# A gated mix of an S5 scan and an H3 convolution on one core: the order of VectorE's products and sums in the convolution chunks, and the place of the inverse transform

## The chip, the core and the metric

The kernel runs on one core of one Trainium2 chip. The metric is device time in microseconds (us) of one execution, the median of several runs. A profiled execution gives beside it a span: the time from the first to the last instruction that the profile shows. Engines are named as the profile names them: PE (TensorE, matmuls), PEld (its weight loads), DVE (VectorE), ACT (ScalarE), POOL (GpSimd), SP (SyncE, which only issues transfers here).

## What is computed

Two sequence models over the same input x (2048 rows of 1024 channels) are mixed by a gate. Cut to what matters:

```python
g = sigmoid((x * gate_w).sum(-1, keepdims=True))
a = S5(x)       # complex linear recurrence h = Lam_bar*h + Bu, then 2*Re(C h) + x*Dskip
# b: H3, per channel
k_shift = 4-tap causal convolution of k with shift_k
kv = k_shift * v
y  = causal convolution of kv with ssm_k over the 2048 rows   (by FFT of length 4096)
b  = x * (y + kv * ssm_D)
out = g * a + (1 - g) * b
```

The change lies in the long convolution, `y`.

## The kernel before

**Two stages.** The convolution stage goes over the 1024 channels in 8 chunks of 128 (`c` = 0 to 7). In it stand also the first pieces of the S5 part (`Bu`, the products of x with B), put between the convolution's steps. The scan stage follows, with 16 scans on DVE, the products with C on PE, and the output rows.

**One chunk.** The 2048 rows are handled as four blocks of 512 and transformed per block by matmuls with cosine and sine tables. For chunk c there are:

- `taps` (line 571): the four taps as matmuls, evicted by ACT into `ks`; `times_v` (line 601) multiplies `ks` by v on DVE, mirrors half of it by a matmul with a reflection matrix (`mirror`, line 579), has ACT evict that to `lo`, forms the even part `ev = ks - lo` on DVE and the odd part by a copy-add of POOL (`gather`, a transfer that adds to its destination) into `ks`.
- `fwd_K` and `fwd_V` (lines 634, 672): the spectra of the filter and of kv, matmuls into PSUM tiles `psk` and `psv`, evicted by ACT into `BT` (the filter's spectrum, K) and `Vh` (V).
- `products` (line 685): the product of the two spectra block by block, so that block a of K meets blocks 0 to 3-a of V. The sum is `A`, which lies in `sums` (named acc in the profile): `A[k, c, b, x]` with k the part of K, c the part of V, b the output block and x 512 frequency-channel pairs. Then the complex combination, and two sums into `whole[c]` (named Vh), which take V's place.
- `inverse` (line 753): for each half `par`, 8 matmuls with the tables CI and SI into a PSUM tile `psz`, an eviction `cv` on ACT, and a store of it to device memory by SP.

**products in detail, chunks 1 to 6.** It is a generator; each `yield` is a place where the main loop goes on with other work. Its steps on DVE:

1. `first(0)`: A[0] = K0 * V, 4096 elements for each partition.
2. `second(0)`: 3072 elements into `WK` (wkh in the profile), and a copy-add of POOL that adds them to A[0].
3. `first(1)`: A[1], 4096.
4. `second(1)`: 3072 into WK.
5. A[1] += that (line 723), 3072.
6. `n2` (4096, into `WK[:, 3072:7168]`, which overlaps what step 5 reads) and `n3` (2048, into a tile `t`).
7. n2 += n3 (2048); A[1] += n2[1] (2048).
8. A[0] += n2[0] (2048).
9. A[1,1] = A[0,0] - A[1,1] and A[1,0] = A[0,1] + A[1,0] (2048 each), then the two sums into `whole[c]` (2048 each).

Chunk 7 runs the same steps without POOL's copy-add, from line 1324; chunk 0 has its own halves.

**What sets the order.** Every instruction is recorded through `put` (line 92), which keeps the order of the program on each engine, so all engines work strictly in the order in which the generators are stepped. `step(g)` runs one piece, `steps(g, n)` n pieces, `run(g)` the rest. All such instructions carry line 94 in the profile, so they are told apart by the names of their tiles. A wait for an earlier instruction of the same engine is a semaphore wait like any other.

**The loop around the change** (lines 1184 to 1197), with c the chunk whose products are formed, n = c + 1 the one whose mirror and `ev` are formed, and c - 1 the one that is transformed back:

```python
step(old); step(tabs)          # turn tables of the S5 part, ACT (c <= 4; old: c 2 to 5)
step(back)                     # first half of inverse(c-1): PE, ACT, store
step(tv)                       # mirror(n) on PE, lo on ACT
steps(prod, 3)                 # first(0), second(0), first(1)
run(tv)                        # ev on DVE, copy-add into ks on POOL
step(prod)                     # second(1)
step(old); step(tabs)
run(back)                      # second half of inverse(c-1)
run(old)
```

`ks` of chunk n is multiplied by v at the end of the turn before (line 1254), right behind the sums into `whole[c-1]`. PSUM has four tiles of two banks, taken in turn by everything that is multiplied.

Of the kernel before, what the change touches and what calls it, by code (L numbers as in the profile page):

```python
# [9 lines left out]
ALU = mybir.AluOpType  # L10
ACT = mybir.ActivationFunctionType
BF16 = mybir.dt.bfloat16
# [8 lines left out]
def kernel(  # L21
# [70 lines left out]
    def put(eng, f, *a, **kw):  # L92
        with tc.issue_after(prev[eng]) if eng in prev else nullcontext():
            i = f(*a, **kw)  # L94
        prev[eng] = getattr(i, "ins", i)
# [4 lines left out]
    def bc(ap, shape):  # L100
        return ap.to_broadcast(shape)
# [3 lines left out]
    def tt(o, a, b, op):  # L105
        put("dve", V.tensor_tensor, out=o, in0=a, in1=b, op=op)
# [19 lines left out]
    def gather(o, i):  # L126
        put("pool", nc.gpsimd.dma_start, out=o, in_=i, accum_op=ALU.add)
# [5 lines left out]
    def h3pool(st, name, bufs, **kw):  # L133
        return st.enter_context(tc.tile_pool(name=name, bufs=bufs, **kw))
# [6 lines left out]
    WK = h3pool(h3, "wkh", 1).tile([128, 7168], BF16, name="wkh")  # L141
# [543 lines left out]
    def products(c, h=0, home=u4, by_dma=True):  # L685

        K, Vt = (x[c][h].rearrange("p c b f d -> p c b (f d)") for x in (KH, VH))
        w = K.shape[3]
        A = sums[:, :, h * 2048:h * 2048 + 8 * w].rearrange("p k (c b x) -> p k c b x", c=2, x=w)

        def mult(a, t):

            if len(t.shape) == 2:
                t = t.rearrange("p (k y) -> p k y", k=2)
            t = t.rearrange("p k (c b x) -> p k c b x", c=2, x=w)
            k_ = bc(K[:, :, a:a + 1], [128, 2, 8 - 2 * a, w])
            v_ = bc(Vt[:, :, 0:4 - a].rearrange("p c b x -> p c (b x)")[:, None], [128, 2, 2, (4 - a) * w])
            tt(t, k_, v_, ALU.mult)
            return t

        n1 = WK[:, h * 3072:h * 3072 + 12 * w].rearrange("p (k c b x) -> p k c b x", k=2, c=2, b=3)

        def first(k):

            for f in range(2 if c == 0 and h == 0 else 1):
                x = slice(f * 128, f * 128 + 128) if c == 0 and h == 0 else slice(0, w)
                tt(A[:, k, :, :, x], bc(K[:, k:k + 1, 0:1, x], [128, 2, 4, x.stop - x.start]), Vt[:, :, :, x], ALU.mult)

        def second(k):
            tt(n1[:, k], bc(K[:, k:k + 1, 1:2], [128, 2, 3, w]), Vt[:, :, 0:3], ALU.mult)  # L710

        if by_dma:
            first(0)
            yield
            second(0)
            gather(A[:, 0, :, 1:], n1[:, 0])
            yield
            first(1)
            yield
            second(1)  # L720
            if c > 0:
                yield
            tt(A[:, 1, :, 1:], A[:, 1, :, 1:], n1[:, 1], ALU.add)
        else:
            mult(0, sums)
            yield
            mult(1, WK[:, 0:6144])
            yield
            tt(A[:, :, :, 1:], A[:, :, :, 1:], n1, ALU.add)
        if c > 0:  # L730
            yield
        n2 = mult(2, WK[:, 3072:7168] if c > 0 else home([128, 8 * w], BF16, "t"))
        n3 = mult(3, home([128, 4 * w], BF16, "t"))
        yield
        tt(n2[:, :, :, 1:], n2[:, :, :, 1:], n3, ALU.add)
        tt(A[:, 1, :, 2:], A[:, 1, :, 2:], n2[:, 1], ALU.add)
        yield
        tt(A[:, 0, :, 2:], A[:, 0, :, 2:], n2[:, 0], ALU.add)
        yield
        tt(A[:, 1, 1], A[:, 0, 0], A[:, 1, 1], ALU.subtract)  # L740
        tt(A[:, 1, 0], A[:, 0, 1], A[:, 1, 0], ALU.add)
        if c == 0 and h == 0:
            return
        t2 = sums[:, 1]
        if c > 0:
            lo, hi = (A[:, 1, :, :, i * 256:(i + 1) * 256] for i in range(2))
        else:
            lo, hi = (t2[:, i * 2048:(i + 1) * 2048].rearrange("p (c b x) -> p c b x", c=2, x=256) for i in range(2))
        to = whole[c].rearrange("p (a c b x) -> p a c b x", a=2, c=2, b=4)
        tt(to[:, 0], lo, hi, ALU.subtract)  # L750
        tt(to[:, 1], lo, hi, ALU.add)
# [326 lines left out]
    def step(gen):  # L1078
        next(gen, None)

    def run(gen):
        for _ in gen:
            pass

    def steps(gen, n):
        for _ in range(n):
            step(gen)
# [59 lines left out]
    for c in range(NC - 1):  # L1147
        n, nn = c + 1, c + 2
        if c == 0:
            load("kn", 2)  # L1150
            load("kT", 2)
            load("v", 2)
            load_BT(0, 0)
            load_xT(0, (0,))
            p1 = products(0, 1)
            fwd_K(n, (0, 1))
            steps(p0, 2)
            run(tv)
            dg = dgs(nn, True)
            steps(p1, 2)  # L1160
            step(p0)
            step(p1)
            run(p0)
            taps(nn, dg)
            step(sp)
            fwd_K(n, (2, 3))
            step(p1)
            step(sp)
            fwd_V(n)
            run(p1)  # L1170
            run(fold_K(nn))
            tv = times_v(nn)
            step(tv)
            load("kn", 3)
            load("kT", 3)
            load_BT(0, 1)
            apart = spread(3)
            step(apart)
            load_xT(0, (1,))
            run(apart)  # L1180
            continue
        if c == 6:
            put("pool", nc.gpsimd.tensor_copy, stamp, xTs[2][:, 0, 0:HB + 1:HB])
        tabs, back, prod = turn_table(c - 1) if c <= NG else none, inverse(c - 1), products(c)
        step(old)
        step(tabs)
        if c == 6:
            step(parts)
        step(back)
        step(tv)  # L1190
        steps(prod, 3)
        run(tv)
        step(prod)
        step(old)
        step(tabs)
        run(back)
        run(old)
        fk = none
        if nn < NC:
            dg = dgs(nn)  # L1200
            if by_channel(nn):
                fk = fold_columns(nn)
                step(fk)
        if c == 2:
            step(parts)
        fwd_K(n, (0, 1))
        if c in (2, 6):
            step(parts)
        fwd_K(n, (2, 3))
        if c == 1:  # L1210
            lam_diag(0, lam_pool, True)
        if c == 4:
            step(parts)
        if c == 6:
            run(sp)
            s5p["Q"] = s5p["wu"]
            run(turns_U[2])
            gate(0)
        step(prod)
        if nn < NC:  # L1220
            if not by_channel(nn):
                fk = mirror_K(nn)
            step(fk)
            if c < 5:
                step(fk)
            if c == 4:
                step(parts)
            if c == 1:
                load_BT(1, 0, True)
            elif c < 5:  # L1230
                load("v", nn, True)
            step(parts)
            taps(nn, dg)
            if c == 5:
                load("v", nn)
                load_xT(2, held=True)
            if nn + 1 < NC:
                load("kT", nn + 1, True)
                load("kn", nn + 1)
                apart = spread(nn + 1)  # L1240
                step(apart)
                if c == 1:
                    load_BT(1, 1)
                elif c in (2, 3):
                    load_xT(1, (3 - c,))
                run(apart)
        step(prod)
        run(fk)
        run(prod)
        if n == NC - 1:  # L1250
            overlap_K(n)
        if nn < NC:
            tv = times_v(nn)
            step(tv)
            step(parts)
        else:
            run(next(tiles))
            CT[0] = ld.tile([128, 2, D], BF16, name="CTa", tag="ld")
            hold(CT[0][:, 0, 0:1])
            load_CT(0)  # L1260
            load_BT(2, 0)
            load_BT(2, 1)
            run(next(tiles))
            run(next(tiles))
        fwd_V(n, (0, 1))
        if c < 6 and c != 4:
            step(parts)
            if c in (1, 3):
                step(parts)
        fwd_V(n, (2, 3))  # L1270
        if c in (4, 5):
            step(parts)
        if c == 1:
            lam_diag(1, lam_pool)
        old = tabs

    h3r.close()
    c = NC - 1
# [38 lines left out]
    with tc.tile_pool(name="fin", bufs=1, side="right") as fin:  # L1317
# [6 lines left out]
        prod, back = products(c, 0, room, False), inverse(c - 1)  # L1324
# [24 lines left out]
    back = inverse(c)  # L1349
# [207 lines left out]
```

## Time and profile before

| | |
|---|---|
| median of 3 runs | 382.99 us (382.91 to 383.02) |
| the profiled execution | 383.41 us |
| its span | 381.6 us |
| granted TensorE clock | 0.997 |
| instructions in the profile | 6664 |

A timeline row gives start, duration, engine, operation, output and inputs by the program's names, their shapes, how many instructions the row stands for, and in brackets the idle time before it and what ended it. Durations of neighbouring instructions may overlap, as their ends are partly modelled; the step from one start to the next is therefore the better measure of what an instruction costs its engine.

### The profile page before, as it was taken

Reading aid. Unit: us, or ns where it says so; the run is one execution under the profiler, and the core shown is the slowest. Engines: PE = TensorE matmul, PEld = TensorE weight load, DVE = VectorE, ACT = ScalarE, POOL = GpSimd, SP = SyncE. Lnnn points to the kernel's source line nnn. Section 1 sums busy time; section 2 is a strip of 40 time slices with the busy share of each in tenths; the row PEclk is TensorE's granted clock in tenths of the full one; section 3 lists DMA queues with packets and bytes.
Section 4 is the critical chain, followed back from the end, with each engine's and each line's share of the span. In section 5 each row is a group of like instructions: output and inputs, shape, how many; then the busy total and the mean of one; then the engine's idle time right before and its main releaser. Section 6 shows DMA issues by size and latency. Waiting matters only on the chain.

```text
span 381.6 us, 6664 instructions
## 1 busy us (share of the span) xinstructions
PE 374.0 (98%) x2469; PEld 201.0 (53%) x2469; DVE 370.8 (97%) x566; ACT 309.5 (81%) x475; POOL 80.3 (21%) x109
## 2 busy tenths in 40 slices
PE   8999999999999999999999999999999999999995
PEld 6656367574674846644454444444444444444434
DVE  8899999999999999999999999999999999999996
ACT  5879998988979998786949999986989669937621
POOL 4011030110301103041002113122415233635000
PEclk9999999999999999999999999999999999999998
DMA  7989999999999998959999999958798999998902
GB/s 167 167 113 260 221 208 185 225 210 223 202 171 197 214 203 188 180 126 154 210 208 209 218 196 210 241 127 143 152 236 162 235 249 229 166 246 142 221 1 110
DMA packets 126259, 71.78 MB, mean 188 GB/s; under 512 B 104649, under 2 KB 107601, under 8 KB 126226
## 3 DMA queue, kind: packets, MB, share of 16 engines
q1 hardware_dynamic: 112416, 45.90, 55.9%
q0 software_dynamic: 12688, 25.17, 39.2%
q8 instruction: 19, 0.31, 0.4%
q10 hardware_dynamic: 1122, 0.28, 0.4%
q14 instruction: 14, 0.11, 0.1%
HBM read 15.48 MB, written 8.39 MB: 63 GB/s over the span
## 4 chain that ended last, share of the span: by engine, by line
DVE 50%; PE 19%; issue 14%; DMA 9%; ACT 5%; POOL 2%; DVEq 0%; POOLq 0%; ACTq 0%
DVE acc L94 14%; DVE wkh L94 9%; PE both L94 9%; DVE A L94 7%; DMA U<-Q 5%; DVE U L94 4%; DMA row<-gd 3%; DVE t L94 3%; DVE trn L94 3%; DVE Vh L94 2%; PE taps L94 2%; PE psz L94 2%; DVE ks L94 2%; ACT Q L94 2%; PE psk L94 2%
## 5 line engine op out<-in xcount | busy, mean ns | idle before, releaser
L94 PE MATMUL psy<-CT,U 128*128 128x512 bf16 (+1 forms) x426 | 93.4, 374 | 0.9 <-DVE U L94 0.9
L94 PEld LDWEIGHTS <-U 128*128 128x128 bf16 x492 | 48.0, 98 | 56.9 <-DVE U L94 1.4
L94 PEld LDWEIGHTS <-BT 128*128 128x128 bf16 x544 | 50.5, 98 | 33.4
L94 ACT ACTIVATE Q<-U,lam 128x512 bf16<-128x512 bf16 (+1 forms) x66 | 39.0, 635 | 15.9 <-DVE U L94 15.9
L94 DVE TENSOR_TENSOR wkh<-BT,Vh 128x3072 bf16<-128x3072 bf16 (+3 forms) x24 | 44.2, 1842 | 0.2
L94 POOL DMA_DIRECT2D U<-Q x26 | 26.1, 1018 | 83.4 <-ACT Q L94 35.7
L94 DVE TENSOR_TENSOR acc<-BT,Vh 128x4096 bf16<-128x4096 bf16 (+3 forms) x19 | 36.9, 1949 | 0.3 <-ACT Vh L94 0.2
L94 PE MATMUL both<-xT,BT 128*128 128x512 bf16 x160 | 35.3, 379 | 0.0
L94 ACT ACTIVATE Vh<-psv 128x1024 bf16<-128x1024 f32 x32 | 30.7, 1032 | 5.5 <-PE psv L94 5.5
L94 ACT ACTIVATE BT<-psk 128x1024 bf16<-128x1024 f32 x31 | 30.3, 1032 | 3.3 <-PE psk L94 3.1
L94 DVE TENSOR_TENSOR acc<-acc,wkh 128x2048 bf16<-128x2048 bf16 (+3 forms) x23 | 32.3, 1431 | 0.5
L94 DVE TENSOR_TENSOR_SCAN A<-rv,init,A 128x256 bf16<-128x256 f32 x48 | 32.2, 731 | 0.0
L94 ACT ACTIVATE U<-both 128x512 bf16<-128x512 f32 x44 | 24.2, 594 | 9.6 <-PE both L94 9.3
L94 POOL DMA_DIRECT2D acc<-wkh x8 | 9.8, 1219 | 103.3 <-DVE wkh L94 103.3
L94 PE MATMUL psk<-eok,SF 128*128 128x384 bf16 (+1 forms) x120 | 28.5, 354 | 0.0
L94 PEld LDWEIGHTS <-SF 128*128 128x128 bf16 x184 | 18.0, 98 | 18.8
L94 PE MATMUL psz<-Vh,CI 128*128 128x512 bf16 x64 | 24.3, 380 | 0.0
L94 PE MATMUL psz<-Vh,SI 128*128 128x512 bf16 x64 | 24.3, 379 | 0.0
L94 PEld LDWEIGHTS <-kT 128*128 128x128 bf16 x352 | 22.2, 103 | 1.3 <-DMA kT<-in_B_k_dram 0.8
L94 PE MATMUL taps<-dg,kT 128*128 128x128 bf16 (+1 forms) x352 | 22.6, 216 | 0.0
L94 PE MATMUL both<-xT,BTl 128*128 128x512 bf16 x96 | 21.2, 379 | 0.0
L94 PE MATMUL both<-BT,BT 128*128 128x512 bf16 x96 | 21.0, 379 | 0.0
(223 smaller groups left out, 770.1 us busy)
## 6 DMA issues: line engine op xcount, KB each, us to landing
U<-Q POOLq DMA_DIRECT2D x26, 256.0 KB, 5.1
acc<-wkh POOLq DMA_DIRECT2D x6, 768.0 KB, 8.6
cv_scr<-cv SPq DMA_DIRECT2D x16, 256.0 KB, 7.5
kn<-in_B_ssm_k_dram SPq DMA_DIRECT2D x5, 512.0 KB, 4.8
v<-in_B_v_dram SPq DMA_DIRECT2D x5, 512.0 KB, 6.1
out_dram<-m SPq DMA_DIRECT2D x8, 256.0 KB, 4.4
BT<-cv_scr SPq DMA_DIRECT2D x7, 256.0 KB, 7.5
out_dram<-BT SPq DMA_DIRECT2D x7, 256.0 KB, 2.0
```

The costliest lines, as they stand in the source:

```text
L94: i = f(*a, **kw)
```

## The change

In `products`, for chunks 1 to 7, steps 6 to 8 are reordered and three instructions are issued in halves: n3 comes ahead of n2; n2's product, the sum n2 += n3, and A[0] += n2[0] are each made as two instructions, one for each k or each c. In the loop, both halves of the inverse now come ahead of the mirror, and `second(1)` comes ahead of `ev`.

```diff
-        n2 = mult(2, WK[:, 3072:7168] if c > 0 else home([128, 8 * w], BF16, "t"))
-        n3 = mult(3, home([128, 4 * w], BF16, "t"))
-        yield
-        tt(n2[:, :, :, 1:], n2[:, :, :, 1:], n3, ALU.add)
-        tt(A[:, 1, :, 2:], A[:, 1, :, 2:], n2[:, 1], ALU.add)
-        yield
-        tt(A[:, 0, :, 2:], A[:, 0, :, 2:], n2[:, 0], ALU.add)
-        yield
+        if c > 0:
+            n3 = mult(3, home([128, 4 * w], BF16, "t"))
+            n2 = WK[:, 3072:7168].rearrange("p (k c b x) -> p k c b x", k=2, c=2, b=2)
+            for k in (1, 0):
+                tt(n2[:, k], bc(K[:, k:k + 1, 2:3], [128, 2, 2, w]), Vt[:, :, 0:2], ALU.mult)
+            yield
+            for k in (1, 0):
+                tt(n2[:, k, :, 1:], n2[:, k, :, 1:], n3[:, k], ALU.add)
+            tt(A[:, 1, :, 2:], A[:, 1, :, 2:], n2[:, 1], ALU.add)
+            yield
+            for i in (0, 1):
+                tt(A[:, 0, i, 2:], A[:, 0, i, 2:], n2[:, 0, i], ALU.add)
+            yield
+        else:
...
         tt(A[:, 1, 1], A[:, 0, 0], A[:, 1, 1], ALU.subtract)
         tt(A[:, 1, 0], A[:, 0, 1], A[:, 1, 0], ALU.add)
...
-        step(back)
+        run(back)
         step(tv)
-        steps(prod, 3)
+        steps(prod, 4)
         run(tv)
-        step(prod)
         step(old)
         step(tabs)
-        run(back)
         run(old)
```

Under `else` chunk 0 keeps the old lines.

More of the change, by code (lines that the diff above doesn't have):

```diff
@@ L731, in products @@
             yield
-        n2 = mult(2, WK[:, 3072:7168] if c > 0 else home([128, 8 * w], BF16, "t"))
-        n3 = mult(3, home([128, 4 * w], BF16, "t"))
-        yield
-        tt(n2[:, :, :, 1:], n2[:, :, :, 1:], n3, ALU.add)
-        tt(A[:, 1, :, 2:], A[:, 1, :, 2:], n2[:, 1], ALU.add)
-        yield
-        tt(A[:, 0, :, 2:], A[:, 0, :, 2:], n2[:, 0], ALU.add)
-        yield
+        if c > 0:
[12 more added lines that the diff above has]
+        else:
+            n2 = mult(2, home([128, 8 * w], BF16, "t"))
+            n3 = mult(3, home([128, 4 * w], BF16, "t"))
+            yield
+            tt(n2[:, :, :, 1:], n2[:, :, :, 1:], n3, ALU.add)
+            tt(A[:, 1, :, 2:], A[:, 1, :, 2:], n2[:, 1], ALU.add)
+            yield
+            tt(A[:, 0, :, 2:], A[:, 0, :, 2:], n2[:, 0], ALU.add)
+            yield
         tt(A[:, 1, 1], A[:, 0, 0], A[:, 1, 1], ALU.subtract)
```

## The prediction

> **What bounds the kernel now.** I read the page's first table, then the list of all waits, then the windows, then the timeline of VectorE (DVE) over one convolution chunk, and last the timelines of the others around the places that the diff moves.
>
> ```profile
> PE 374.0 (98%) x2469; PEld 201.0 (53%) x2469; DVE 370.8 (97%) x566; ACT 309.5 (81%) x475; POOL 80.3 (21%) x109
> ```
> ```profile
> PEld L94 <- DVE ks L94: 4.4, 6, 0.9
> ...
> PE mirror L94 <- DVE ks L94: 1.5, 4, 0.4
> ...
> PEld L94 <- DVE Vh L94: 1.2, 3, 0.5
> PE psy L94 <- DVE U L94: 0.9, 1, 0.9
> ```
> ```profile
> 240.00:270.00 30.00, 30.00 (x140) 13.55 (x139) 29.62 (x64) 25.06 (x39) 6.19 (x8) 1.00 0.82 168
> ```
>
> The reader is to see two full engines. The windows row is one from the second half (stretch and length, then PE, weight load, DVE, ACT and POOL busy): PE 30.00 of 30 us, DVE 29.62. The waits list says which of the two holds the other. Behind the start, DVE has no row in it against another engine; PE has these four against DVE. So DVE sets the end, PE follows it closely, and what counts is whether DVE loses time between its own instructions. It does:
>
> ```profile
> 92.11 1.22 DVE L94 TENSOR_TENSOR ks<-ks,v 128x2048 bf16<-128x2048 bf16 x1
> 93.24 2.29 DVE L94 TENSOR_TENSOR acc<-BT,Vh 128x4096 bf16<-128x4096 bf16 x1
> 95.44 1.75 DVE L94 TENSOR_TENSOR wkh<-BT,Vh 128x3072 bf16<-128x3072 bf16 x1
> 97.11 2.29 DVE L94 TENSOR_TENSOR acc<-BT,Vh 128x4096 bf16<-128x4096 bf16 x1
> 99.32 0.69 DVE L94 TENSOR_TENSOR ev<-ks,lo 128x1024 bf16<-128x1024 bf16 x1
> 99.92 1.75 DVE L94 TENSOR_TENSOR wkh<-BT,Vh 128x3072 bf16<-128x3072 bf16 x1
> 101.71 1.76 DVE L94 TENSOR_TENSOR acc<-acc,wkh 128x3072 bf16<-128x3072 bf16 x1
> 103.50 2.29 DVE L94 TENSOR_TENSOR wkh<-BT,Vh 128x4096 bf16<-128x4096 bf16 x1
> 105.71 1.22 DVE L94 TENSOR_TENSOR t<-BT,Vh 128x2048 bf16<-128x2048 bf16 x1
> 106.96 1.22 DVE L94 TENSOR_TENSOR wkh<-wkh,t 128x2048 bf16<-128x2048 bf16 x1
> 108.22 2.36 DVE L94 TENSOR_TENSOR acc<-acc,wkh 128x2048 bf16<-128x2048 bf16 x2
> 110.62 2.36 DVE L94 TENSOR_TENSOR acc<-acc 128x2048 bf16<-128x2048 bf16 x2
> 113.01 2.36 DVE L94 TENSOR_TENSOR Vh<-acc 128x2048 bf16<-128x2048 bf16 x2
> 115.29 1.22 DVE L94 TENSOR_TENSOR ks<-ks,v 128x2048 bf16<-128x2048 bf16 x1
> ```
>
> This is chunk 3, 23.18 us from ks to ks. Look at starts, not durations. Where the next instruction does not need this one, it starts 0.08 us before this one's end: 3072 elements from 95.44 to 97.11, 1.67 us; 2048 from 92.11 to 93.24, 1.13. Where it does, it starts 0.03 us after the end: 3072 from 99.92 to 101.71, 1.79; 2048 from 105.71 to 106.96, 1.25. **A direct dependence costs 0.12 us**, a loss that no busy column shows. The starts at 101.71, 103.50 (wkh is overwritten while the sum has just read it), 106.96, 108.22, 110.62 and 113.01 are the six such places of the chunk.
>
> **The change, part by part.** *Size of a split.* From 99.32 to 99.92 a 1024-element instruction takes 0.60 us, a 2048 one 1.13: two halves are 1.20, so each split adds 0.07. The diff splits three instructions of 7 chunks (1 to 7): 21 x 0.068 = 1.43 us more on DVE, which nothing hides.
>
> *Gaps closed.* Behind the change ev stands between the second product of wkh and the sum that reads it; t's product stands between that sum and the overwriting of wkh; each half of n2 and each half sum has its sibling between it and its reader; both halves of the last sum into A[0] stand so that A[1,1] reads the older one. Of the six dependent starts only the one into Vh is left. Does one instruction in between suffice? Chunk 5 has that case already:
>
> ```profile
> 152.07 1.22 DVE L94 TENSOR_TENSOR t<-BT,Vh 128x2048 bf16<-128x2048 bf16 x1
> 153.20 0.69 DVE L94 TENSOR_TENSOR eok<-kn,lo 128x1024 bf16<-128x1024 bf16 x1
> 153.81 1.22 DVE L94 TENSOR_TENSOR wkh<-wkh,t 128x2048 bf16<-128x2048 bf16 x1
> ```
>
> wkh<-wkh,t reads t, eok of 1024 elements lies between, and the steps are 1.13 and 0.61: no gap. The shortest instruction between a writer and its reader in the new order is such a 1024 one, so I count these gaps as closed. Chunks 1 to 4 close five each, 0.595; chunk 5 four (one was covered by eok), chunk 6 four (the small state-parameter operations already stood ahead of its sum), chunk 7, which has no ev, four, 0.476 each. Net of the 0.204 for the splits: 4 x 0.39 + 3 x 0.27 = **2.37 us less on DVE**.
>
> The Trainium skill speaks against this ("VectorE: DVE Perf Modes", The DRAIN you can't avoid, and its rules for kernel authors): the next operation waits for the pipe to empty whether or not a semaphore stands between, and one should minimize the count of operations, not of semaphores. The 0.12 us between the two kinds of step disagree with the first half here; the 0.07 per extra instruction agrees with the second. What the change would be if the rule held is a rival below.
>
> *Inverse ahead of the mirror.* PE ahead of chunk 5's mirror, and at the first inverse matmul of chunk 3:
>
> ```profile
> 138.78 0.38 PE L94 MATMUL psz<-Vh,CI 128*128 128x512 bf16 x1
> 139.00 0.38 PE L94 MATMUL psz<-Vh,SI 128*128 128x512 bf16 x1
> 139.75 0.60 PE L94 MATMUL mirror<-ks,refl 128*128 128x512 bf16 x2 [0.37 <-DVE ks L94]
> ```
> ```profile
> 90.51 0.59 PE L94 MATMUL psv<-ks,SF 128*128 128x512 bf16 x2
> 91.11 0.39 PE L94 MATMUL psz<-Vh,CI 128*128 128x512 bf16 x1
> ```
>
> A 512-column matmul takes a slot of 0.22 us (138.78 to 139.00). From 139.00 to 139.75 PE loses 0.53 waiting for ks, of which the row shows 0.37, since a matmul's modelled 0.38 us outlasts its slot by 0.16. The waits list has four such (1.5 us in all on PE) among the six of the weight loads; the other two are hidden in that 0.16. So 4 x 0.53 + 2 x 0.16, about 2.5 us. With both halves of the inverse in front, 16 slots or 3.45 us lie between Vh's first half and the mirror, while ks comes 2 x 1.13 us after that half: the mirror waits no more, and the second Vh half (1.13 after the first) is there when its 8 slots begin. PE also waits for Vh itself 0.17 at 91.11 (two matmuls of 0.22 from 90.51, so it was free at 90.94) which I count twice, 0.3 us, for the list's three waits on Vh; that goes if DVE gains. In all PE can shed 2.8 us.
>
> What is late next on PE? Two things. First, ACT's order becomes cv, cv, lo:
>
> ```profile
> 95.48 1.04 ACT L94 ACTIVATE cv<-psz 128x1024 bf16<-128x1024 f32 x1
> 96.38 1.05 ACT L94 ACTIVATE lo<-mirror 128x1024 bf16<-128x1024 f32 x1
> 97.29 1.06 ACT L94 ACTIVATE cv<-psz 128x1024 bf16<-128x1024 f32 x1
> ```
>
> Four PSUM tiles rotate, so the second psk of fwd_K needs the first cv evicted. Its place is 25 slots or 5.4 us after the first psz (16 psz, 2 mirror, and psk's 4 of 512 and 4 of 384 columns), 96.3 if psz starts at 90.9, and cv ends at 96.5. So some 0.2 us come back in chunk 3, 0.1 in chunk 4, where ACT has the turn tables ahead of cv. For ev nothing changes: lo ends one eviction later, 98.3 instead of 97.4, and ev starts at 100.99 instead of 99.32, since the 1.67 us product passes it.
>
> Second, POOL's copy-add into ks waits for ev, and so is issued 1.67 us later; behind it on POOL stands the turn table's copy-add, used in the next chunk. In chunks 1 and 3:
>
> ```profile
> 50.16 1.20 POOL L94 DMA_DIRECT2D acc<-wkh  x1 [14.70 <-DVE wkh L94]
> 52.96 0.91 POOL L94 DMA_DIRECT2D ks<-lo  x1 [1.61 <-DVE ev L94]
> ```
> ```profile
> DMA to landing us min/median/max: 9.7/9.7/9.7
> ```
> ```profile
> DMA to landing us min/median/max: 8.9/8.9/8.9
> ```
> ```profile
> 97.50 1.20 POOL L94 DMA_DIRECT2D acc<-wkh  x1 [16.08 <-DVE wkh L94]
> 100.31 0.90 POOL L94 DMA_DIRECT2D ks<-lo  x1 [1.61 <-DVE ev L94]
> ```
> ```profile
> DMA to landing us min/median/max: 8.5/8.5/8.5
> ```
> ```profile
> DMA to landing us min/median/max: 7.1/7.1/7.1
> ```
> ```profile
> 62.12 0.59 PE L94 MATMUL psv<-ks,SF 128*128 128x512 bf16 x2
> ```
>
> The landing rows are for acc and ks of chunk 1, then of chunk 3. acc lands at 50.16 + 9.7 = 59.9 and ks at 52.96 + 8.9 = 61.9; in chunk 3 106.0 and 107.4: ks comes 1.4 to 2 us behind acc, though issued 2.8 us later. It queues behind acc's bytes, so I take its landing as unchanged by the later issue (bounds: unchanged, or 1.67 later). In chunk 1 its reader at 62.12 has only 0.3 us in hand; PE arrives 0.5 earlier there and gives back 0.3 with the latencies. PE is left with 2.8 - 0.3 - 0.3 = 2.2 us.
>
> SP's and POOL's queues keep their order; the two cv stores move with their evictions.
>
> *Sum.* DVE comes 2.37 us earlier to the end, if PE and what PE feeds keep pace; PE comes 2.2 us earlier, and has 0.9 us of waiting for DVE at the end besides (psy <- U). Where scans wait for PE's products, 2.2 decides, else 2.37; I take 2.2. The profiled execution took 383.41 us (span 381.6 and 1.8 around it), 0.4 above the median of 382.99. 381.2 for a profiled one, **380.8 us** for the median.
>
> **Rivals.** *Transfers and evictions keep their own pace* (0.20). ks lands 0.3 us ahead of its reader in chunk 1, and ACT is 81% busy. If landings do not move up with their consumers, PE's lead is eaten where the slack is smaller, and DVE is then held by PE, so about half is kept: -1.1, 381.9 us. For it: slacks of tenths. Against: most issues are released by PE, DVE and ACT themselves, so they move too.
>
> *The later ks copy-add lands later* (0.10). If it is not queueing behind acc, it lands at 63.5 in chunk 1, where PE wants it at 61.6: 1.9 us of stall. PE then keeps 2.8 - 1.9 - 0.3 = 0.6 us at most, later chunks may take some of it too, and the scans wait for what PE feeds: -0.5, 382.5. Against it: the 1.4 us between landings for 2.8 us between issues.
>
> *Slower: the gap is paid per instruction or per wait, not per neighbour* (0.07). Then 21 more instructions cost 1.43 us on the engine that sets the end: 384.4 us. It decides where fewer than two of a chunk's gaps close, since 0.204 / 0.119 = 1.7. For it: nearly every new instruction still carries a wait on DVE's own counter. Against it: the eok step of chunk 5. The skill's rule named above would give this case.
>
> *The change does not do what it says*, as the halves end up dependent neighbours: read from the built order, each has another between; no chance of its own. The rest (0.03), slower, is for what I have not seen.
>
> **How the numbers follow.** Forecast 0.60, with its own range 380.4 to 381.3 (-2.6 to -1.7); rivals as given. A measurement of this kernel can tell about 0.2%, 0.77 us, from no change: 382.2. Faster: 0.60 and 0.16 of the first rival's 0.20; same: its other 0.04 and the second's 0.10; slower: 0.07 + 0.03. The range reaches from 380.1 (all 2.8 of PE's waits turned into time) to 382.4, and leaves out the slow cases and part of the second rival.
>
> **What would show it.** In the new DVE timeline a chunk takes 22.8 us from ks to ks, with one 1.25 step, at Vh; 602 ns for each half. The mirror's rows lose "<-DVE ks". psv<-ks in chunk 1 may show a short wait for the copy-add. DVE's instructions are 587, and its busy time rises by some 3 us (2 x 0.69 - 1.22 = 0.16 for each split) although the span falls to 379.4: busy time is no guide here. The prediction is wrong if DVE gets waits for PE or ACT, or if steps behind halves stay at 0.72 (0.60 + 0.12).

## The result, and the profile after

The changed kernel takes 382.23 us in the median of its runs (from 380.27), the kernel before 383.14 us beside it (from 382.79). The ratio is 0.9957, with a 95% interval of 0.9943 to 0.9971: 0.43% or 1.65 us faster, where the prediction had 2.2 us. Executions from 389 us up occur with either kernel and are left out of the ratio, though not of the medians. The others fall in two groups, eight from 380.27 to 381.06 and nine from 382.10 to 383.27; the kernel before has no such groups here. The profiled execution took 380.88 us, of which its span is 379.1. So in the lower group the change is worth about 2.6 us (middle of the eight 380.5, of the kernel before 383.1), in the upper one half a microsecond.

The page's first row of the changed kernel, busy time of each engine:

```profile
PE 370.4 (98%) x2434; PEld 200.2 (53%) x2469; DVE 369.4 (97%) x587; ACT 309.0 (82%) x475; POOL 79.3 (21%) x109
```

DVE has its 587 instructions, 21 more than before, and is busy 1.4 us less. The timeline of DVE over chunk 3 of the changed kernel, from ks to ks:

```profile
90.70 1.22 DVE L94 TENSOR_TENSOR ks<-ks,v 128x2048 bf16<-128x2048 bf16 x1
...
97.91 1.75 DVE L94 TENSOR_TENSOR wkh<-BT,Vh 128x3072 bf16<-128x3072 bf16 x1
99.58 0.69 DVE L94 TENSOR_TENSOR ev<-ks,lo 128x1024 bf16<-128x1024 bf16 x1
100.18 1.75 DVE L94 TENSOR_TENSOR acc<-acc,wkh 128x3072 bf16<-128x3072 bf16 x1
101.85 1.22 DVE L94 TENSOR_TENSOR t<-BT,Vh 128x2048 bf16<-128x2048 bf16 x1
102.98 2.35 DVE L94 TENSOR_TENSOR wkh<-BT,Vh 128x2048 bf16<-128x2048 bf16 x2
105.25 1.28 DVE L94 TENSOR_TENSOR wkh<-wkh,t 128x1024 bf16<-128x1024 bf16 x2
106.46 2.42 DVE L94 TENSOR_TENSOR acc<-acc,wkh 128x2048 bf16<-128x2048 bf16 x3
108.80 2.35 DVE L94 TENSOR_TENSOR acc<-acc 128x2048 bf16<-128x2048 bf16 x2
111.18 2.36 DVE L94 TENSOR_TENSOR Vh<-acc 128x2048 bf16<-128x2048 bf16 x2
113.46 1.22 DVE L94 TENSOR_TENSOR ks<-ks,v 128x2048 bf16<-128x2048 bf16 x1
115.12 2.29 DVE L94 TENSOR_TENSOR acc<-BT,Vh 128x4096 bf16<-128x4096 bf16 x1 [0.44 <-ACT Vh L94]
```

Read the starts. From 90.70 to 113.46 the chunk takes 22.76 us, against 23.18 before. The 3072-element sum now steps 1.67 (100.18 to 101.85) instead of 1.79; the 1024-element ev, which stands between the product into wkh and the sum that reads it, takes 0.60; two halves of 1024 take 1.21 together (105.25 to 106.46). One dependent step is left, into Vh: 2.38 for two instructions of 1.13 and 1.25 (108.80 to 111.18). The last row is new: ahead of chunk 4's products DVE now waits 0.44 us for ACT's eviction of Vh. Before the change chunks 1 to 7 had no such wait.

On PE the waits for DVE at the mirror are gone. The matmul timeline ahead of chunk 5's mirror, in the changed kernel:

```profile
139.77 0.38 PE L94 MATMUL psz<-Vh,SI 128*128 128x512 bf16 x1
139.98 0.59 PE L94 MATMUL mirror<-ks,refl 128*128 128x512 bf16 x2
```

The mirror follows the inverse by one slot, 0.21 us. What holds PE and DVE now is in the changed kernel's list of waits (us in total, times, longest):

```profile
PEld L94 <- DMA kT<-in_B_k_dram: 1.5, 2, 1.1
...
PEld L94 <- DVE U L94: 1.1, 1, 1.1
...
PEld L94 <- DMA kT<-kT: 0.7, 2, 0.5
DVE acc L94 <- ACT Vh L94: 0.7, 2, 0.4
...
PE psv L94 <- DMA ks<-lo: 0.3, 1, 0.3
PE taps L94 <- DMA kT<-kT: 0.2, 1, 0.2
```

The rows "<- DVE ks" (4.4 and 1.5 us before) have gone. The first row above does not take their place: its two waits end at 4.55 and 7.05 us, ahead of everything that the change touches, and the kernel before waits 0.8 us there too. New in the chunks are waits for the shifted copy of kT (kT<-kT) and for the copy-add into ks. The shifted copy in chunk 3, on SP's queue in the kernel before, then in the changed one, and then on the changed kernel's PE:

```profile
86.65 2.15 SPq L94 DMA_TRANSPOSE kT<-in_B_k_dram  x1
...
92.11 4.79 SPq L94 DMA_TRANSPOSE xT<-in_A_x_dram  x1
97.02 0.51 SPq L94 DMA_DIRECT2D kT<-kT  x1
```
```profile
85.76 3.48 SPq L94 DMA_TRANSPOSE kT<-in_B_k_dram  x1
...
92.63 4.75 SPq L94 DMA_TRANSPOSE xT<-in_A_x_dram  x1
97.49 0.53 SPq L94 DMA_DIRECT2D kT<-kT  x1
```
```profile
104.52 0.23 PE L94 MATMUL taps<-dg,kT 128*128 128x64 bf16 x2 [0.21 <-DMA kT<-kT]
```

The copy stands behind a transposed load that takes SP 4.75 us. The load of kT is released 0.9 us earlier than before, but takes SP 1.3 us longer, so the copy is issued 0.47 later, while PE comes to the taps 0.9 earlier (105.42 before). A transfer that had room now ends last, by 0.21 us. Such waits are short; what they cost is taken up below.

**Where the time went, by stretches.** I compare profiled executions from Vh of chunk 0 on, since its start scatters from 41.87 to 43.56 us over nine profiles (both kernels, and e1, e3 to e7 and e10 of the experiments below), whatever the kernel. The steps from Vh to Vh of the seven chunks, in us, and what follows the eighth Vh:

| | chunks 1 to 7 | sum | behind |
|---|---|---|---|
| before | 23.18, 24.16, 23.18, 23.18, 23.66, 24.06, 25.24 | 166.66 | 172.5 |
| after | 22.76, 23.74, 22.76, 23.30, 23.43, 23.76, 24.95 | 164.70 | 172.5 |
| after again (e3) | 22.76, 23.73, 22.76, 22.76, 23.37, 23.76, 24.95 | 164.09 | 172.4 |
| after, third (e10) | 22.75, 23.94, 23.60, 23.19, 23.43, 23.76, 24.94 | 165.61 | 172.2 |

All of the gain is in the chunks: 0.42 each in chunks 1 to 4 where nothing stalls, 0.3 in 6 and 7. Without a stall on DVE it is 2.57 us (e3). The execution above loses 0.6 of it, nearly all in chunk 4 with its 0.44 us wait, the third one 1.5. Against that, e3 starts late: its first Vh comes at 43.37 us, 1.45 us behind the execution above (41.92), so that its eighth Vh is 0.84 us later in spite of the shorter chunks.

### The profile page after: what moved, and what is told of

Same layout as the page of the kernel before. It is cut to its first block, busy times and chain, and to the rows that moved or that the text cites. A ratio compares the mean times of both kernels' runs of the same rounds, so it can differ in the third digit from the quotient of the medians.

```text
span 379.1 us, 6655 instructions
## 1 busy us (share of the span) xinstructions
PE 370.4 (98%) x2434; PEld 200.2 (53%) x2469; DVE 369.4 (97%) x587; ACT 309.0 (82%) x475; POOL 79.3 (21%) x109
## 4 chain that ended last, share of the span: by engine, by line
DVE 57%; DMA 15%; PE 12%; issue 9%; ACT 3%; SPq 2%; POOL 1%; DVEq 0%; POOLq 0%
DVE acc L94 13%; DVE A L94 12%; DVE wkh L94 8%; DVE U L94 7%; DVE trn L94 4%; DMA U<-Q 4%; DMA kT<-in_B_k_dram 3%; PE taps L94 2%; PE psk L94 2%; DVE Vh L94 2%; DMA BT<-cv_scr 2%; DVE t L94 2%; PE psv L94 2%; DMA ks<-lo 2%; DMA kT<-kT 2%
## 5 line engine op out<-in xcount | busy, mean ns | idle before, releaser
L94 DVE TENSOR_TENSOR wkh<-BT,Vh 128x2048 bf16<-128x2048 bf16 (+3 forms) x31 | 44.6, 1458 | 0.0
L94 DVE TENSOR_TENSOR acc<-acc,wkh 128x1024 bf16<-128x1024 bf16 (+4 forms) x30 | 32.7, 1129 | 0.1
L94 PE MATMUL taps<-dg,kT 128*128 128x128 bf16 (+1 forms) x352 | 21.6, 209 | 0.6 <-DMA kT<-in_B_k_dram 0.4
L94 PEld LDWEIGHTS <-kT 128*128 128x128 bf16 x352 | 20.8, 99 | 2.7 <-DMA kT<-in_B_k_dram 1.5
```

## The experiments

**The order of DVE alone, and the order of the loop alone.** e1 has the changed products in the loop of before, e2 the products of before in the changed loop.

```diff
-        run(back)
+        step(back)
         step(tv)
-        steps(prod, 4)
+        steps(prod, 3)
         run(tv)
+        step(prod)
         step(old)
         step(tabs)
+        run(back)
```

That is e1, against the changed kernel; e2 is the other half of the diff undone.

> The order and the halves on VectorE alone, the loop as before (mirror between the halves of the inverse, ev ahead of second(1)). My theory (VectorE sets the end, a directly dependent neighbour costs 0.12 us, a split 0.07): one gap less is closed per chunk than in the whole change, so chunks are 23.18 - 4 x 0.12 + 0.20 = 22.9 us from ks to ks, VectorE comes about 1.8 us earlier to the scans, about 381.3 us if nothing else holds it. Rival (the gain comes from TensorE's order): within 0.3 us of 383.0. The mirror's waits for ks stay (1.5 us on PE).

> The loop alone: whole inverse ahead of the mirror and second(1) ahead of ev, products as before. My theory: VectorE closes one gap per chunk (0.12 us, chunks 1 to 5: 0.6 us) and TensorE's 2.5 us of waiting for ks only turn into waiting for Vh, so about 382.4 us, chunks of 23.06 us. Rival (TensorE's order carries the gain): 381 us or less.

e1: 382.79 us, ratio 0.9968 (0.9946 to 0.9989), lowest 381.18. e2: 383.29 us, ratio 0.999 (0.997 to 1.001), lowest 382.45. The kernel before had 383.68 beside them, from 382.68. DVE in chunk 3 of e1 shows the one gap that its loop leaves open:

```profile
100.38 1.75 DVE L94 TENSOR_TENSOR wkh<-BT,Vh 128x3072 bf16<-128x3072 bf16 x1
102.16 1.76 DVE L94 TENSOR_TENSOR acc<-acc,wkh 128x3072 bf16<-128x3072 bf16 x1
103.84 1.22 DVE L94 TENSOR_TENSOR t<-BT,Vh 128x2048 bf16<-128x2048 bf16 x1
```

From 100.38 to 102.16 is 1.78, into the sum that reads wkh; from there to t 1.68. A chunk of e1 without a stall takes 22.89 us, 0.29 less than before. In e2 it takes 23.04 from ks to ks in chunk 3 and 23.05 in chunk 1, 0.13 less (its profiled execution took 392.75 us, so only such steps of it are read):

```profile
91.75 1.22 DVE L94 TENSOR_TENSOR ks<-ks,v 128x2048 bf16<-128x2048 bf16 x1
...
114.79 1.22 DVE L94 TENSOR_TENSOR ks<-ks,v 128x2048 bf16<-128x2048 bf16 x1
```

Both parts fell within 0.02 us of what the count of gaps gives, and 0.29 + 0.13 = 0.42 is the whole. In time, the loop alone can't be told from no change, although it takes all the mirror's waits from PE. So PE's 2.5 us at the mirror were worth nothing that can be told; DVE's steps are what counts. The two ratios do not show this by themselves, since their intervals overlap; the steps do. But e1's order on DVE also met stalls: PE waited 1.65 us for kT<-kT ahead of the taps in chunk 5, and DVE 0.45 and 0.20 for Vh in chunks 3 and 4.

**The whole change again, and without the halves.** e3 is the changed kernel itself, e4 the same order with the three instructions left whole:

```diff
-            n2 = WK[:, 3072:7168].rearrange("p (k c b x) -> p k c b x", k=2, c=2, b=2)
-            for k in (1, 0):
-                tt(n2[:, k], bc(K[:, k:k + 1, 2:3], [128, 2, 2, w]), Vt[:, :, 0:2], ALU.mult)
+            n2 = mult(2, WK[:, 3072:7168])
             yield
-            for k in (1, 0):
-                tt(n2[:, k, :, 1:], n2[:, k, :, 1:], n3[:, k], ALU.add)
+            tt(n2[:, :, :, 1:], n2[:, :, :, 1:], n3, ALU.add)
...
-            for i in (0, 1):
-                tt(A[:, 0, i, 2:], A[:, 0, i, 2:], n2[:, 0, i], ALU.add)
+            tt(A[:, 0, :, 2:], A[:, 0, :, 2:], n2[:, 0], ALU.add)
```

> The changed kernel once more. The first 20 times of it lie in two groups, near 380.5 and near 382.5, while the kernel before stays within 0.5 us. Theory: behind the change transfers (the shifted copy of k into kT, the copy-add into ks) land just when TensorE wants them, so small differences in their landing decide between the groups; then the times scatter over 380.3 to 383.3 again and a profile of the upper group shows longer waits of PE and VectorE for kT, ks or Vh in the chunks. Rival (the granted clock): the upper group shows a lower clock and the same waits.

> The whole change without the halves: n3 ahead of n2, ev behind second(1), the new loop, but n2, its sum and the sum into A[0] in one instruction each. My theory: of the five gaps two are closed (both of WK), three stay, and no split is paid: 23.18 - 0.24 = 22.94 us a chunk against 22.76 with halves, 1.6 us less on VectorE in all, about 381.4 us. Rival (a split costs more than the gap that it closes): faster than the whole change.

e3: 382.15 us, ratio 0.9951 (0.9922 to 0.9979), lowest 380.53. Here the times do not fall in two groups: nine lie between 380.53 and 383.97, four of them from 381.3 to 382.1. The profiled execution, 381.70 us, has no wait of DVE for Vh in chunks 1 to 7. e4: 383.78 us, ratio 0.9988 (0.9957 to 1.0018), lowest 381.46. DVE in e4's chunk 3:

```profile
92.67 1.22 DVE L94 TENSOR_TENSOR ks<-ks,v 128x2048 bf16<-128x2048 bf16 x1
...
104.95 2.28 DVE L94 TENSOR_TENSOR wkh<-BT,Vh 128x4096 bf16<-128x4096 bf16 x1
107.27 1.23 DVE L94 TENSOR_TENSOR wkh<-wkh,t 128x2048 bf16<-128x2048 bf16 x1
108.53 2.36 DVE L94 TENSOR_TENSOR acc<-acc,wkh 128x2048 bf16<-128x2048 bf16 x2
...
115.60 1.22 DVE L94 TENSOR_TENSOR ks<-ks,v 128x2048 bf16<-128x2048 bf16 x1
```

The whole product steps 2.32 into its sum, the whole sum 1.26 into its reader, both with the gap. The chunk is 22.93 us, 0.17 longer than with the halves, although it has three instructions fewer. So the halves pay: three splits at 0.07 buy three gaps at 0.12, 0.153 by the prediction's numbers. That settles the rival of a gap paid per instruction, on DVE; the median of e4 itself, whose interval reaches from 0.9957 to 1.0018, would not have. In time e1 and e4 fell short of what had been expected of them: 1.2 us (0.32%) instead of 1.8, and 0.5 us instead of 1.6, although e4's seven steps sum to 165.15 us, 1.51 less than before. Their profiles start late as well, with the first Vh at 43.01 and 43.56 us.

**Do two transfers hold PE?** What was left to explain is why the change as a whole gains less than the 2.6 us of the lower group. My theory was that the shifted copy of kT makes the upper group of times, through taps, psv and Vh; the rival, that it is something else. e5 leaves out that copy (chunks 3 to 7) and the copy-add into ks (chunks 2 to 7), e6 does the same in the kernel before, e7 leaves out the shifted copy alone.

```diff
-        move(a[hi, 10:], a[lo, 8:n - 2])
...
-        else:
-            gather(ks[:, 2:4], lo)
```

> The changed kernel, leaving out two transfers of each chunk on which TensorE was seen to wait: the last shifted copy of k into kT's upper half (chunks 3 to 7), and the copy-add of lo into ks (chunks 2 to 7), so its taps and odd parts lack these terms. Theory (behind the change these landings hold TensorE, and through Vh at times VectorE): no PE wait on kT or ks in the chunks, every chunk 22.76 us, the times close together at the floor of the changed kernel, 380 to 380.6 us. Rival (the scatter comes from elsewhere, the start or the scans): the same 380.3 to 383.3 as with them.

> The kernel before, leaving out the same two transfers. Theory: its chunks of 23.18 us leave these landings room, so it gains nothing of note, 382.7 to 383.3 us, within 0.3 us of the kernel before on the same chip. Rival (transfers were the bound all along, and the order on VectorE a detail): as fast as the changed kernel without them.

> The changed kernel, leaving out only the last shifted copy of k into kT (chunks 3 to 7). It tells the two landings apart: if kT is the one that matters, it is as close and as fast as without both; if it is the copy-add into ks, the scatter of the changed kernel stays, with PE waiting up to 1.6 us at psv<-ks in chunk 1 or 5.

e5: 380.83 us (380.15 to 381.28), ratio 0.9938 (0.9921 to 0.9956). e7: 380.50 (380.20 to 381.29), ratio 0.9934 (0.9917 to 0.9951). e6: 382.85, ratio 1.0003 (0.9987 to 1.002). Before the change, then, these transfers bounded nothing. After it, with them left out, all executions lay below 381.3 us, which looked like the theory. It is not shown, as e10 below tells: on another occasion the whole changed kernel stayed below 381.6 us too. Nor did e5 go below the lower group, and with neither transfer in it DVE still waited for Vh in chunks 3 and 4, 0.51 and 0.34 us.

**More room for the copy.** If the copy is late because SP issues a transposed load of 4.75 us ahead of it, the load can go behind it:

```diff
                 step(apart)
+                run(apart)
                 if c == 1:
                     load_BT(1, 1)
                 elif c in (2, 3):
                     load_xT(1, (3 - c,))
-                run(apart)
```

> The changed kernel, with the last shifted copy of k issued ahead of the transposed load (xT or BT) that stands before it on SP's queue in chunks 2 to 4. In the changed kernel that copy was issued at 97.49, behind the load's 4.75 us on the queue and 6.0 us behind kB's copies, and 4.9 us behind them in chunk 5, where no load stands between. Theory: about 1 us more room for the taps of the chunks after it, none for chunk 5's wait, so the median comes down by some tenths towards 381, the floor stays. Rival: the load, issued later, is late itself, and the time gets longer by up to 1 us.

393.84 us, ratio 1.0284 (1.0248 to 1.0321): 11 us slower than the kernel before. SP's queue, the landing of POOL's copy-add into acc (issued at 96.5), and DVE, in e8's chunk 3:

```profile
96.36 0.46 SPq L94 DMA_DIRECT2D kT<-kT  x1
96.87 3.70 SPq L94 DMA_TRANSPOSE xT<-in_A_x_dram  x1
```
```profile
DMA to landing us min/median/max: 19.1/19.1/19.1
```
```profile
115.72 1.29 DVE L94 TENSOR_TENSOR acc<-acc,wkh 128x1024 bf16<-128x1024 bf16 x2 [7.61 <-DMA acc<-wkh]
```

The copy went out 1.1 us earlier, but the transposed load now left the queue beside the copy-add, and what was issued around and behind it landed late: acc after 19.1 us, against 7.5 in the changed kernel, where the load is issued 3.5 us ahead of it; ks after 16.6 against 6.5; SP's two stores of cv after 16.8 against 6.6 in the median. DVE waited 7.61 us, PE 9.06 for ks. PE was slower behind it, too: the granted clock is 0.50 from 112.6 to 120 us, and the first two psv, from 117.66, take 1.01 us instead of 0.59. In chunk 4 DVE waits another 3.10 us for Vh, so that its two waits make up 10.7 of the 11.1 us by which e8's span (390.2) exceeds the changed kernel's (379.1). The theory fell, and the rival, which had allowed it 1 us, was far too low as well. The Trainium skill ("DMA: Bandwidth & Descriptors", Issuing engines are not separate DMA queues) says that transfers of all issuing engines run on the same 16 DMA engines and interleave; e8's landings agree, for SP's stores and POOL's copy-adds alike. Why a transposed load holds the others by this much, no run here shows.

**An earlier load, and the whole change a third time.** e9 issues the load of kT ahead of the taps, with a tile of its own for kB; e11 has that tile alone; e10 is the changed kernel.

```diff
+    kb_pool = h3pool(h3r, "kb", 1, side="right")
...
-                lds["kB", c] = ld.tile([128, PAD + S], BF16, name="kB", tag="ld")
+                lds["kB", c] = kb_pool.tile([128, PAD + S], BF16, name="kB", tag="kb")
...
+            if nn + 1 < NC:
+                load("kT", nn + 1, True)
             taps(nn, dg)
...
             if nn + 1 < NC:
-                load("kT", nn + 1, True)
                 load("kn", nn + 1)
```

> The changed kernel complete, with kB in a buffer of its own and the load of the next k therefore issued ahead of the taps instead of behind them (chunks 4 to 7), about 3 us earlier in the chunk. Theory (kT's chain of load, copy and shifted copy, which starts when the taps before have freed the buffer, is as long as the shorter chunk): with 3 us more room the taps do not wait, the upper group of times goes, about 380.6 us in the median. Rival (the transposed load now runs beside POOL's copy-adds and delays them, as the later load of xT did): longer, by up to some us, with PE or VectorE waiting for acc or ks.

> The changed kernel with kB in a buffer of its own, all loads where they were. Theory: the load of k still stands behind the taps in the order, so nothing of note moves: the changed kernel's times, within 0.3 us. If it is as good as the early load, the room and not the place of the load is what counts.

> The changed kernel once more, on the chip of the run with the early load, as its measure. Theory: times from 380.3 to 383, in two groups; waits of PE on kT or ks in the profile. If it lies at 380.6 throughout, the groups belong to the chip and not to the kernel.

e9: 385.50 us, ratio 1.0069 (1.0043 to 1.0095), slower. e11: 383.40 us, ratio 1.0005 (0.9978 to 1.0033), lowest 380.37. e10: 380.52 us (380.17 to 381.52), ratio 0.9936 (0.9915 to 0.9958). The kernel before had 382.95 beside them. PE in chunk 5, first of e9, then of e11:

```profile
157.38 0.59 PE L94 MATMUL psv<-ks,SF 128*128 128x512 bf16 x2 [3.84 <-DMA ks<-lo]
```
```profile
155.68 0.61 PE L94 MATMUL psv<-ks,SF 128*128 128x512 bf16 x2 [3.49 <-DMA ks<-lo]
```

More room for kT moves its load (in chunk 4 to 131.31 and 131.96 us on SP's queue, from 132.68), and another transfer comes late: the copy-add into ks lands 10.0 and 9.5 us after its issue, against 6.2 in the changed kernel. e11, from which nothing of note had been expected, spreads from 380.37 to 385.79 us. Neither is a version to keep. And e10, with no upper group at all, shows short waits too. First PE of e10 in chunk 1, then its DVE at the start of the products of chunks 3 and 4:

```profile
56.23 1.91 PE L94 MATMUL odd<-xT,BT 128*128 128x256 bf16 x16 [0.88 <-ACT lamd L94]
58.61 0.23 PE L94 MATMUL taps<-dg,kT 128*128 128x64 bf16 x2 [0.47 <-DMA kT<-kT]
```
```profile
92.81 2.29 DVE L94 TENSOR_TENSOR acc<-BT,Vh 128x4096 bf16<-128x4096 bf16 x1 [0.75 <-ACT Vh L94]
...
116.00 2.29 DVE L94 TENSOR_TENSOR acc<-BT,Vh 128x4096 bf16<-128x4096 bf16 x1 [0.34 <-ACT Vh L94]
```

The first PE row names ACT, but the same instruction in e5 and e7 waits for the load of xT. From start to start these two cost PE 1.04 and 0.64 us, a modelled end hiding 0.16 of each. Two chunks later DVE waits. I put the same two places of the other profiles that have the changed order on DVE beside it (us, from start to start in both rows, less the steps without a wait):

| | e3 | e4 | e7 | after | e1 | e5 | e10 |
|---|---|---|---|---|---|---|---|
| PE's waits for transfers in chunk 1 | 0 | 0 | 0.43 | 0.56 | 0.91 | 1.27 | 1.68 |
| DVE's waits for Vh in chunks 3 and 4 | 0 | 0 | 0.18 | 0.53 | 0.81 | 1.02 | 1.27 |

The order is the same in both rows. PE, 98% busy, doesn't make up what it loses in chunk 1; it comes late with psv, ACT late with Vh, and DVE pays 40 to 95% of it. Which transfer was late in chunk 1 differs: xT in e5 and e7, kT's copy in e1, that and ks in the changed kernel's first profile. (There the 0.38 us ahead of chunk 3's taps is in neither row.) The seven profiles agree on this; no run forces it, since none delays one transfer alone. A rival stands untested: e3 and e4, the two without waits, are also the two that start latest (43.37 and 43.56 us), so a late start of DVE may be what gives the transfers their room.

e10's profile is of the execution of 381.52 us, the longest of its six. So stalls for late transfers go with a spread of about one microsecond, and so, by e3, does a late start. The upper group is not explained: no profile of the changed kernel fell in it, and it was absent on e10's occasion, as it was for e5 and e7 on theirs. A late start, 1.45 to 1.64 us later in e3 and e4 than in the changed kernel's first profile, could make most of the 2 us between the groups. So could a long wait of PE with a slower clock behind it, as in e9 and e11: behind the waits shown above, their granted clock is 0.57 (158 to 162 us) and 0.77 (154 to 158), and 0.995 in the mean of either; four of the nine executions of the upper group have means of 0.994 to 0.997, while none of the lower group is below 0.998. Neither is shown. Since e7 and e10 gain the same, each beside the kernel before (0.9934 and 0.9936), leaving out the shifted copy is worth nothing that could be measured.

## Why the prediction was right, and by how much it was off

*DVE sets the end, PE follows closely.* Held. The change of DVE's order alone (e1) brought 0.32%, the loop with PE's freedom (e2) nothing that can be told.

*A direct dependence costs 0.12 us, a split 0.07, and one instruction of 1024 elements in between suffices.* Held to 0.03 us a chunk. Predicted 0.39 in chunks 1 to 4 and 0.27 in 5 to 7; measured without stalls (e3) 0.42 and 0.3; in all 2.57 against 2.37 us. e4 against e3 has three gaps more and three splits less and is 0.17 longer, so the three splits cost 3 x 0.12 less 0.17, 0.19, where 0.204 had been counted.

*The slower rival, a gap for each instruction or wait.* Fell. By it chunk 3 would have grown by 3 x 0.07, to 23.4; it shrank to 22.76. The Trainium skill's section that the prediction named for it ("VectorE: DVE Perf Modes", The DRAIN you can't avoid: the next operation waits for the pipe to empty, with or without a semaphore) does not fit these rows, taken as the prediction took it. The section adds that a next operation which is not held starts earlier, which the prediction left out. In the rows it is the dependence that decides: behind the 3072-element product of wkh comes the next start after 1.67 us where ev stands ahead of its reader (97.91 to 99.58), after 1.78 in e1 where the reader itself is next. The rule to keep the count of operations low would have been wrong here, with 587 instructions faster than 566.

*The mirror no longer waits.* Held: no "<- DVE ks" is left on PE. But PE's 2.8 us were not what limited the result, since e2 sheds them without a gain.

*What comes late next.* The wait of chunk 3's second psk for the first eviction of cv was put at 0.2 us. In the changed kernel's matmul timeline two psk of 384 columns start at 95.13, and the next starts at 95.67:

```profile
95.13 0.49 PE L94 MATMUL psk<-eok,NCF 128*128 128x384 bf16 x2
95.67 0.59 PE L94 MATMUL psk<-eok,CF 128*128 128x512 bf16 x2
```

Two slots of 0.16 end at 95.45, so PE lost 0.22. The copy-add's reader in chunk 1 was put at 0.3 us of wait; the row of the list shows 0.3 (0.42 from start to start). Both sizes held, the second roughly. *Its landing* was taken as unchanged by the later issue. In chunk 3 it landed at 100.56 + 6.5 = 107.1, against 107.4 before, but the whole chunk began 1.41 us earlier, so this is no proof. Counted from the issue of acc's copy-add, it landed after 11.8, 11.3, 11.0, 11.1, 10.7 and 7.9 us in chunks 1 to 6, against 11.7, 10.0, 9.9, 11.8, 9.8 and 7.9 before, and after 11.1, 9.8, 9.8, 12.1, 11.4 and 7.9 in e3. For an issue 1.67 us later that is 0.4 and 0.2 us more in the mean, with 0.7 less to 1.6 more in single chunks. It held in the mean, and in chunk 1, where the second rival had put 1.9 us of stall; in single chunks it was luck.

*The sum, "if PE and what PE feeds keep pace".* This is the step that was too large. The forecast kept 2.2 us; the ratio gives 1.65, just short of the forecast's own range (1.7 to 2.6), and the median came to 382.23 us where 380.8 had been forecast. PE fed DVE late through Vh in two of the three profiles, which lost 0.6 and 1.5 us: waits of DVE for ACT, which the prediction had named as a sign of its being wrong. That the profiled span met the forecast (379.1 us, 379.4 foretold) is luck, as that execution belongs to the lower group. The first rival named the mechanism (transfers keep their own pace, so about half is kept: 381.9), and the truth lies between it and the forecast. What I had not priced were SP's transfers, the load of xT and the shifted copy of kT: the copy-adds and the evictions had been looked at, SP's queue had only been said to "keep" its order, and no landing on it was set against its reader. How much of the missing 0.9 us (2.57 less 1.65) these stalls make, how much the start, which the prediction took as fixed, and how much whatever divides the times in two groups, stays open.

*Busy time of DVE up by 3 us.* Wrong: it fell by 1.4. The busy column counts overlapping time once, as one row of the changed kernel's groups shows:

```profile
L94 DVE TENSOR_TENSOR wkh<-BT,Vh 128x2048 bf16<-128x2048 bf16 x14 | 16.5, 1217 | 0.0
```

14 x 1.217 is 17.0, yet the group is busy 16.5. The overlap of 0.08 us of each pair of halves is not counted twice, so adding durations for new instructions overstates the busy time. And each closed gap takes some away: of its 0.12 us 0.03 had been idle, and about 0.09 is busy time that neighbours now share. By that estimate 32 closed gaps take away 2.9 us and 21 splits add 1.4, which is the change that was measured. The warning that busy time is no guide here was right for a reason that I had not seen.

## What to carry to other kernels

On an engine that sets the end, read steps from start to start, sort them by whether the next instruction needs this one, and count the dependent ones: here each was worth 0.12 us, and even splitting an instruction in halves, at 0.07, paid when the halves then stood between a writer and its reader. Before counting on such a gain, list for every transfer how long ahead of its reader it lands, in each chunk, since one with some tenths to spare becomes the next wait. Moving such a transfer forward can cost far more than it saves, if it brings a transposed load beside copies that others wait for.

## What the runs showed that I had not expected

- A transposed load issued 0.35 us behind a copy-add, instead of 3.5 us ahead of it, made that copy-add land after 19.1 us instead of 7.5 (e8); the order of two lines in the program cost more than the whole change had gained, and left the kernel 11 us slower than before.
- PE, when it is busy throughout, seems to carry a wait for a transfer over two chunks: 1.68 us lost in chunk 1 went with 1.27 us of DVE's waits in chunks 3 and 4 (e10), and the other profiles rank alike; no run delays one transfer alone.
- The start of the kernel, up to the first Vh of DVE, scatters by 1.7 us between executions (41.87 to 43.56). Two profiles whose spans differ by less say nothing until they are compared from a common instruction on.
- The same changed kernel has two groups of times on one occasion (380.3 to 381.1 and 382.1 to 383.3), a spread without a gap on another (e3) and little more than the lower group on a third (e10); the mean granted clock is 1.000 in some executions of either group, so it alone does not tell them apart.
